# A written order of 800 steps, ordered anew: linear attention and a channel mix on one core

## The chip, the cores and the metric

The kernel runs on one core of a Trainium2 chip. The metric is the device time of one execution in microseconds. The kernel before took 197.18 us (median of three runs, 197.18 to 197.22).

## The reference, cut to what matters

```python
def _attn_ref(q, k, v, g_norm):            # q, k, v: (8, 8, 576, 64) = batch, head, token, channel
    kv = np.einsum('bhsd,bhse->bhde', k, v)
    out = np.einsum('bhsd,bhde->bhse', q, kv)
    rms = np.sqrt(np.mean(out * out, axis=-1, keepdims=True) + 1e-06)
    return out / rms * g_norm

def _moe_ref(x, mu_k, mu_r, w_k, w_v, w_r):  # x: (8, 576, 512), w_k: (512, 1024), w_v: (1024, 512), w_r: (512, 512)
    x_prev = np.concatenate([np.zeros((B, 1, D)), x[:, :-1, :]], axis=1)
    xk = mu_k * x + (1.0 - mu_k) * x_prev
    xr = mu_r * x + (1.0 - mu_r) * x_prev
    k = np.maximum(xk @ w_k, 0.0)
    v = k * k @ w_v
    r = 1.0 / (1.0 + np.exp(-(xr @ w_r)))
    return r * v

def reference(**kwargs):                   # x is the attention's output, heads side by side in the channels
    ...
```

## The kernel before

Every batch goes through two halves. The attention half makes `kv` from k and v, turns q, multiplies them (`u`), squares and reduces the result, takes a reciprocal root (`rs`), multiplies by it, and turns the result into `xT`, with channels on the partitions. The channel-mix half forms the difference of neighbouring tokens (`dx`), scales it by `mu_k` or `mu_r` (`m`), adds `x` (`xk`, `xr`), and runs three large products: `K` (`xk` by `w_k`, relu, square), `R` (`xr` by `w_r`, sigmoid) and `V` (the squares by `w_v`). Two batches together make nine tiles of 128 tokens for `R` and `V`.

The order of all this is written out by hand or by a search: `ORDER` is one list of some 800 words, and a loop at the end of the kernel calls one function for each (`name.arguments`). A planner takes no part (`manual_schedule`); each engine runs its instructions in the list's order, and waits where data or a buffer isn't ready. An apostrophe puts the step on VectorE (DVE), otherwise it goes to ScalarE (ACT), where there is a choice. Digits behind `=` choose the PSUM banks that the step takes, of eight; a bank is taken again only after the step that empties it.

The words that matter below:

- `cast`, `kvc`, `kvco`, `qtc`, `qtco`, `uc`, `sqc`, `msc`, `rsc`, `mcc`: the attention half of batch 0, which has code of its own (cast the first loads; kv on TensorE (PE) and its evacuation; q's transposes and their evacuation; the product; its square; the means by a matmul; the root; the product with the root into `xT`).
- `cols`: a transpose of the rows with `mu_k`, `mu_r` and `g_norm` into columns, and its copy on DVE.
- `wm.n.i`: n matmuls on zeros into a bank that nobody reads; they keep PE busy. Another 12 stand ahead of the list.
- `dif`, `difh`, `dih`: the difference; `sc`: the scale by `mu` (`sc.b.0.h` for `xk`, `sc.b.1.h` for `xr`); `fu`: scale and addition in one; `add`, `adda`: the addition.
- `Ka`, `Kz`: `K` of batch 0's later tokens, in two halves of the contraction; `Kz` ends with the relu. `Kp.b.j.n`: `K` for other parts of batches 0 and 1 (`Kp.0.1` are the "low units", the first 256 tokens of batch 0). `K.b.f.h`: from batch 2 on. `ksp`, `ks`: the square of the relu's result.
- `qt`, `qto`, `kvh`, `kvho`, `uh`, `sqh`, `redh`, `rsh`, `mulh`, `xh`, `xho`, `x0h`, `x0ho`: batch 1's attention, in two halves of the heads (the last digit, 0 or 1).
- `kv`, `kvo`, `kvs`, `u`, `sq`, `red`, `nw`, `mul`, `x`, `xo`, `x0`, `x0o`, `wrap`: the attention of later batches; `qd` and `yd`: transposes by DMA on SP's queue, from batch 3 and 4 on; `gx`: the scale by `g_norm`.
- `R`, `V`, `Vq` (half a `V` step), `fin`, `fip`, `sta`, `L`: the products, their last multiplication and the stores.
- `ld.n.b`: the load of k, v or q (n = 0, 1, 2) of batch b on GpSimd's queue. The loads of batches 0 and 1 and of the weights are issued ahead of the list, in a fixed order.

```python
    for period in ORDER:
        for word in period.split():
            word, _, digits = word.partition("=")
            chosen[:] = map(int, digits)
            name, *args = word.rstrip("'").split(".")
            ops[name](DVE if word.endswith("'") else ACT, *map(int, args))
```

Of the kernel before, what the change touches and what calls it, by code (L numbers as in the profile page):

```python
# [31 lines left out]
    ld.1.2 Kp.0.1.2=1 mulh.1.1.0 xh.2.2.0=56 x0h.0=32 Kz.0.5 mulh.1.0.0 x0ho.0.1 xh.0.2.0=74 ksp.0.1.0.4'
    Vq.0.1.0=1 xho.0.2.0.0 sc.0.1.2 sc.0.1.0' xho.2.2.0.1' ksp.0.1.4.8' Vq.0.0.0=0 xho.0.2.0.1 xho.2.2.0.0'
    qt.1.1=62 kvh.1=75 qto.1.1.1 Vq.0.1.1 kvho.1.0 x0ho.0.0' qto.1.1.0' kvho.1.1 Vq.0.0.1 uh.0.1=34 ld.2.3
    ksp.0.0.4.8' uh.1.1=62 uh.2.1=7 Vq.0.3.0=5 sqh.0.1.1 add.0.1.0 sqh.0.0.1 Vq.0.3.1 ld.1.3 add.0.1.1 sqh.1.1.1
    sqh.2.0.1 sqh.1.0.1 redh.5.9.1 rsh.5.9.1 redh.0.5.1 rsh.0.5.1 Vq.0.3.2 tab ld.0.3 mulh.0.0.1 Vq.0.0.2
    mulh.0.1.1 Vq.0.3.3 Vq.0.1.2 mulh.2.0.1 Vq.0.0.3 xh.2.2.1=34 mulh.1.1.1 mulh.1.0.1 xho.2.2.1.0' xho.2.2.1.1
    Vq.0.1.3 xh.0.2.1=72 x0h.1=63 xho.0.2.1.0 xho.0.2.1.1 wrap.1 x0ho.1.0' x0ho.1.1' R.0.3=4 dif.1.384.576
    dif.1.0.384 sc.1.0.3.384.576 R.0.2=6 sc.1.0.1.0.384' sc.1.0.2.384.576' sc.1.0.1.384.576 R.0.0=3 qt.2.0=72
    sc.1.1.0' qt.2.1=46 sc.1.0.3.0.384' sc.1.0.2.0.384' sc.1.0.0.0.384' qto.2.1.0 qto.2.1.1 sc.1.0.0.384.576'  # L40
    R.0.1=3 adda.1.0.384.576 add.1.0.0.0.384 add.1.0.1.0.384 Kp.1.0.2'=4 qto.2.0.1' Kp.1.0.3'=6 Kp.1.1.1=3
    Vq.0.2.0=4 ld.2.4 fin.0.1 Vq.0.2.1 fin.0.3 sc.1.1.1 add.1.1.0 Vq.0.2.2 Kp.1.1.2=2 qto.2.0.0' fin.0.0
    sc.1.1.3' Vq.0.2.3 qd.3 sc.1.1.2' Kp.1.1.3'=6 Kp.1.1.0=3 Kp.1.1.5'=1 kv.2=57 ksp.1.1.0.2 kvo.2.0' kvo.2.1'
    Kp.1.1.4=2 u.2.2=0 u.2.1=63 sq.2.2.0 add.1.1.1 sq.2.1.0 u.2.0=15 sq.2.1.1 Kp.1.0.0=7 sq.2.0.0 sq.2.0.1 qd.4
    ksp.1.1.2.4' ld.0.4 ld.1.4 Kp.1.1.7=2 fin.0.2 red.2.0.5 R.1.4=4 red.2.5.9 Kp.1.1.6=7 Kp.1.0.1=2 R.1.5=4
    ksp.1.1.4.6' ld.2.5 nw.2.0.1 V.1.5.0=7 nw.2.1.2 nw.2.2.3 ksp.1.1.6.8 nw.2.3.4 nw.2.4.5 R.1.7=2 V.1.4.0=4
# [8 lines left out]
    K.2.1.1=0 nw.3.2.3 sc.2.1.1' K.2.4.1=3 K.2.4.0=6 nw.3.3.4 K.2.7.0=0 nw.3.4.5 ks.2.5' K.2.1.0=3 nw.3.5.6
    sc.2.1.2 nw.3.6.7 nw.3.7.8 mul.3.1.1 mul.3.2.0 K.2.6.0=6 ks.2.1 K.2.6.1=0 V.1.8.0=3 K.2.2.1=6 mul.3.1.0
    K.2.3.0=5 mul.3.0.1 mul.3.0.0 add.2.1.1 add.2.1.0 K.2.2.0'=1 K.2.7.1=0 K.2.0.0=7 x0.3=65 ks.2.6 x.3.0.4=42
    V.1.8.1 xo.3.0.4.1 x0o.3.1 R.2.0=0 ks.2.3 xo.3.0.4.0' ks.2.2' x0o.3.0' ks.2.4' wrap.3 R.2.3=7 ks.2.7 R.2.2=1
    ks.2.0' dif.3 sc.3.0.3' sc.3.0.1 V.2.0.0=4 kv.4=25 V.2.2.0=6 V.2.2.1 fin.1.8 sc.3.1.3' kvo.4.1' sc.3.0.0'
# [7 lines left out]
    K.3.2.0=7 ks.3.7' ks.3.1' kvo.5.1 add.3.1.1 V.2.3.0=1 K.3.5.0=6 K.3.6.0=2 V.2.3.1 yd.4 kvs.5.1 K.3.5.1=3
    ks.3.2' kvs.5.0 sc.3.1.1' K.3.3.1=5 K.3.3.0=7 u.5.0=06 sq.5.0.1 sq.5.0.0 fin.2.1 u.5.1=24 u.5.2=3 sq.5.1.0
    sq.5.2.0 add.3.1.0 fin.2.3 sq.5.1.1 R.3.6=1 R.3.4=5 ks.3.3' R.3.8=7 V.3.7.0=1 ks.3.6' red.5.5.9 red.5.0.5
    nw.5.0.1 V.3.6.0=5 ks.3.5 ld.0.6 nw.5.1.2 nw.5.2.3 nw.5.3.4 nw.5.4.5 nw.5.5.6 nw.5.6.7 V.3.6.1 nw.5.7.8  # L70
    mul.5.2.0 gx.4.1 mul.5.1.0 V.3.7.1 V.3.4.0=7 ld.1.6 mul.5.1.1 gx.4.0 mul.5.0.0 R.3.5=3 mul.5.0.1 wrap.4
# [770 lines left out]
```

## Time and profile before

| | |
|---|---|
| median of three runs | 197.18 us |
| the profiled execution's own time | 197.49 us |
| its span, first to last instruction | 195.7 us |
| TensorE busy | 186.0 us, 2316 records of matmuls |
| VectorE busy | 160.1 us, 349 instructions |
| ScalarE busy | 133.8 us, 279 instructions |
| GpSimd busy | 30.7 us |
| moved by DMA | 32.75 MB, mean 167 GB/s |

A busy share is time in which at least one instruction of the engine was under way. Matmuls overlap: one of 512 columns shows 379 ns, and twenty in a row take 4.3 us. A few matmul records are missing from the trace, so counts in the groups are a little low. A row of the timeline gives start, length, engine, line, operation, output and inputs, count, and in brackets the idle time of the engine ahead of it and what ended it. Columns of the table of stretches: length, then busy time and count of PE, PE's weight loads, DVE, ACT and GpSimd, then granted clock, DMA share and GB/s.

### The profile page before, as it was taken

The numbers are of one execution on the slowest core, as the hardware profiler recorded it, in microseconds if no ns is written. First come the engines' busy times: TensorE is split into PE (matmuls) and PEld (weight loads), VectorE is DVE, ScalarE is ACT, GpSimd is POOL, SyncE is SP. The second block draws the span as 40 slices with busy tenths as digits, with TensorE's granted clock in tenths as the row PEclk, the third lists the DMA queues.
The fourth block names the chain that finished last, engine by engine and source line by source line (L and its number), as shares of the span: only waits on it lengthen the run. The fifth ranks groups of instructions, "written<-read, shape, count | busy, mean of one in ns | idle before, by whom it ended". The sixth has DMA issues, their size and how long they took to land.

```text
span 195.7 us, 5668 instructions
## 1 busy us (share of the span) xinstructions
PE 186.0 (95%) x2316; PEld 110.5 (56%) x2343; DVE 160.1 (82%) x349; ACT 133.8 (68%) x279; POOL 30.7 (16%) x50
## 2 busy tenths in 40 slices
...
GB/s 220 212 211 205 195 208 205 208 209 230 233 177 166 147 224 228 206 246 211 183 169 141 188 173 160 225 179 85 186 169 73 87 138 0 54 55 109 54 153 170
DMA packets 42958, 32.75 MB, mean 167 GB/s; under 512 B 23852, under 2 KB 37428, under 8 KB 42932
## 3 DMA queue, kind: packets, MB, share of 16 engines
...
## 4 chain that ended last, share of the span: by engine, by line
PE 56%; DVE 30%; ACT 5%; issue 3%; DMA 3%; SPq 1%; DVEq 0%
PE ps_km L634 21%; PE ps_v L676 17%; PE ps_r L666 11%; DMA rows<-in_g_norm_dram 3%; DVE yd L401 3%; DVE sqk L642 2%; DVE xr L621 2%; PE ps_kv L288 1%; DVE y__1281 L423 1%; PE ps_km L725 1%; DVE xT L515 1%; DVE ss__1215 L363 1%; PE ps_u L318 1%; DVE ss__2860 L363 1%; DVE ss__1583 L363 1%
## 5 line engine op out<-in xcount | busy, mean ns | idle before, releaser
L676 PE MATMUL ps_v<-wv_sb,sqk 128*128 128x512 bf16 x265 | 64.4, 379 | 1.4 <-issue 0.8
L634 PEld LDWEIGHTS <-wk_sb 128*128 128x128 bf16 x480 | 45.8, 98 | 16.8 <-issue 0.5
L676 PEld LDWEIGHTS <-sqk 128*128 128x128 bf16 x280 | 26.6, 98 | 28.8
L666 PE MATMUL ps_r<-wr_sb,xr 128*128 128x512 bf16 x135 | 35.2, 379 | 0.6
L666 PEld LDWEIGHTS <-xr 128*128 128x128 bf16 x144 | 13.8, 98 | 14.3 <-DVE xr L621 0.2
L626 ACT ACTIVATE rt<-ps_km 128x384 bf16<-128x384 f32 (+2 forms) x18 | 8.8, 506 | 7.0 <-PE ps_km L634 4.2
L261 PE MATMUL ps_warm<-zeros 128*128 128x512 bf16 x25 | 9.4, 501 | 1.2 <-DVE eps L224 1.2
L634 PE MATMUL ps_km<-xk__3239,wk_sb 128*128 128x288 bf16 x64 | 9.0, 286 | 0.0
L634 PE MATMUL ps_km<-xk__968,wk_sb 128*128 128x192 bf16 (+1 forms) x64 | 8.8, 286 | 0.0
L634 PE MATMUL ps_km<-xk__2666,wk_sb 128*128 128x288 bf16 x64 | 8.8, 286 | 0.0
L634 PE MATMUL ps_km<-xk__3386,wk_sb 128*128 128x288 bf16 x64 | 8.7, 286 | 0.1
L634 PE MATMUL ps_km<-xk__2429,wk_sb 128*128 128x288 bf16 x64 | 8.7, 286 | 0.0
L634 PE MATMUL ps_km<-xk__1923,wk_sb 128*128 128x288 bf16 x64 | 8.7, 286 | 0.0
L634 PE MATMUL ps_km<-xk__1557,wk_sb 128*128 128x288 bf16 x64 | 8.4, 286 | 0.1
L428 ACT ACTIVATE xT<-xT,cols 128x1152 bf16<-128x1152 bf16 x6 | 7.3, 1266 | 0.1
L515 DVE SCALAR_TENSOR_TENSOR xT<-ps_u,cols,rs 128x384 bf16<-128x384 f32 x6 | 3.7, 613 | 3.1 <-ACT rs L511 3.1
L725 PE MATMUL ps_km<-xk__371,wk_sb 128*128 128x320 bf16 x32 | 5.4, 299 | 0.7 <-DVE xk__371 L610 0.4
L261 PEld LDWEIGHTS <-zeros 128*128 128x128 bf16 x28 | 3.0, 117 | 5.0 <-issue 3.1
...
L428 ACT ACTIVATE xT<-ps_x,cols 128x256 bf16<-128x256 bf16 (+3 forms) x10 | 5.2, 563 | 0.4 <-PE ps_x L438 0.4
...
L642 DVE TENSOR_TENSOR sqk<-rt 128x1280 bf16<-128x1280 bf16 (+3 forms) x7 | 5.1, 722 | 0.0
...
## 6 DMA issues: line engine op xcount, KB each, us to landing
...
```

The lines of the kernel that those rows point to most:

```text
L261: nc.tensor.matmul(ps, zeros[:, :128], zeros, start=True, stop=True)
L363: DVE.tensor_reduce(out=ss[:, g0:g1], in_=sq[:, g0:g1], op=ALU.add, axis=AX.X)
L401: DVE.tensor_mul(out=pairs[:, :, i, 1 + t0:1 + t0 + n].rearrange("p c t x -> p t c x"), in0=u_, in1=by)
L428: eng.activation(out=dst, in_=src, func=AF.Copy, scale=g_sb)
L515: DVE.scalar_tensor_tensor(out=xT[0][:, hps, P + c0:P + c1], in0=give(("uc", key)), scalar=g_sb, in1=rs0[:, hps, c0:c1], op0=ALU.mult, op1 ...
L621: DVE.tensor_add(out=dst, in0=m[:, hs, c0:c1], in1=x[:, hs, c0:c1])
L626: eng.activation(out=dst, in_=ps, func=AF.Relu)
L634: nc.tensor.matmul(ps[:, n, :], wk_sb[:, cc, 128 * fc:128 * fc + 128], at[b]["xk"][:, cc, c0:c1], start=(cc == 0), stop=(cc == NHP - 1))
L642: eng.tensor_mul(out=sqk[:, fcs, o:o + n], in0=src, in1=src)
L666: nc.tensor.matmul(ps, xr[:, cc, 128 * t:128 * t + 128], wr_sb[:, cc, :], start=(cc == 0), stop=(cc == NHP - 1))
L676: nc.tensor.matmul(ps, sqk[:, fc, 128 * t:128 * t + 128], wv_sb[:, fc, :], start=(fc == 0), stop=(fc == NFC - 1))
L725: nc.tensor.matmul(ps[:, n, :], wk_sb[:, cc, 128 * fc:128 * fc + 128], at[0]["xk"][:, cc, c0:c1], start=(cc == 0), stop=(cc == NHP - 1))
```

## The change

Only `ORDER` differs. The same steps stand in another order, with other banks, and some steps change between DVE and ACT (60 go to DVE, 58 to ACT over the whole list). No matmul, no other operation and no load is added or taken away but for the warming matmuls: 28 before, 26 after. The loads that stand in the list change places within it: v of batch 2 now goes ahead of k of batch 2, k of batch 3 ahead of v of batch 3, and so on. Line numbers below the list grow by one.

The start of the list, before and after (the rest is ordered anew in the same manner, up to the last two steps, `L.0` and `L.1`):

```diff
-    cast.1' cast.0 kvc.0.2=01 cols=2 kvco.0 qtc.0.2=34 kvco.1 qtco.0' qtco.1 wm.2.0=2 uc.0=5 qtc.2.2=67
+    cast.0' cast.1' kvc.0.2=01 kvco.0 wm.1.0=7 qtc.0.2=23 kvco.1' qtco.0' qtco.1 cols=4 wm.1.1=1 uc.0=5 sqc.0
+    uc.1=6 qtc.2.2=70 msc.0=1 sqc.1 msc.1=2 wm.1.2=3 kvc.2.1=4 kvco.2' qtco.2 rsc.0 wm.1.3=1 uc.2=3 rsc.1 uc.4=7
+    qtco.3' wm.1.4=0 kvc.3.1=1 kvco.3 sqc.2 wm.1.5=0 uc.3=4 mcc.1 mcc.0 difh.0.0.256.576 sc.0.0.0.256.576' sqc.3
+    uc.5=2 sqc.5 msc.2=0 sc.0.0.1.256.576' rsc.2 wm.1.6=1 msc.3=6 rsc.3 sqc.4 msc.5=5 ld.2.2 add.0.0.0.256.576
+    mcc.2 dih.0.2.256.576 wm.4.7=1 Ka.0.7=1 msc.4=0 rsc.4 Ka.0.4=6 mcc.3 fu.0.0.2.256.576 dih.0.3.256.576
+    Ka.0.6=3 Ka.0.5=4 fu.0.0.3.256.576 Ka.0.0=0 rsc.5
...
-    sqc.0 uc.1=0 ld.2.2 sqc.1 qtco.2 msc.0=1 wm.2.1=4 msc.1=2 rsc.0 kvc.2.1=3 kvco.2 wm.2.2=6 uc.2=4 uc.4=6
-    rsc.1 mcc.1 qtco.3' mcc.0 difh.0.0.256.576 kvc.3.1=1 sqc.2 sqc.4 sc.0.0.1.256.576' sc.0.0.0.256.576' msc.2=3
-    kvco.3 wm.1.3=0 uc.3=2 msc.4=0 uc.5=1 sqc.3 rsc.4 msc.3=7 add.0.0.0.256.576 wm.4.4=5 Ka.0.0=5 rsc.3 sqc.5
-    mcc.3 Ka.0.5=0 rsc.2 dih.0.3.256.576 mcc.2 fu.0.0.3.256.576 mcc.4 msc.5=7 rsc.5 Ka.0.4=2 Ka.0.6=3 Ka.0.2=4
-    dih.0.2.256.576 fu.0.0.2.256.576 mcc.5 Ka.0.1=7 wrap.0 difh.0.0.0.256 Ka.0.7=6 difh.0.1.0.256 fu.0.0.3.0.256
-    Kz.0.4 Kz.0.0 Kz.0.1' Ka.0.3=1 Kz.0.3' fu.0.0.1.0.256 Kz.0.6 wm.2.5=5 qt.1.0=25 qto.1.0.1 Kz.0.2 Kz.0.7
-    fu.0.0.2.0.256 wm.2.6=1 kvh.0=37 kvho.0.1 qto.1.0.0' sc.0.1.1' kvho.0.0' fu.0.0.0.0.256 wm.1.7=6 uh.0.0=15
-    uh.1.0=42 sqh.0.1.0 sqh.1.1.0 sc.0.1.3' uh.2.0=6 ksp.0.0.0.4' sqh.0.0.0 sqh.1.0.0 sqh.2.0.0 redh.5.9.0
...
+    ld.1.2 Ka.0.3=5 Kz.0.0 mcc.5 Kz.0.4 Kz.0.6 Kz.0.5 Ka.0.1=2 wrap.0 mcc.4 Kz.0.3 difh.0.0.0.256 difh.0.1.0.256
+    fu.0.0.3.0.256 fu.0.0.1.0.256 Kz.0.7 fu.0.0.2.0.256 fu.0.0.0.0.256 sc.0.1.1 Ka.0.2=0 Kz.0.2 Kz.0.1'
+    qt.1.0=76 sc.0.1.3 qto.1.0.0 wm.1.8=1 Kp.0.1.1=3 qto.1.0.1' sc.0.1.2 kvh.0=45 ksp.0.0.0.4' kvho.0.1'
+    kvho.0.0' wm.2.9=7 uh.2.0=1 sqh.2.0.0 uh.1.0=02 uh.0.0=67 sqh.1.1.0 ksp.0.0.4.8' sqh.1.0.0 sc.0.1.0'
+    redh.0.5.0 sqh.0.0.0 Kp.0.1.0=5 sqh.0.1.0 ksp.0.1.0.4' rsh.0.5.0 mulh.2.0.0 redh.5.9.0 Kp.0.1.3=3 mulh.1.0.0
+    Kp.0.1.2=4 mulh.1.1.0 Vq.0.1.0=5 Vq.0.1.1 Vq.0.0.0=1 xh.0.2.0=34 rsh.5.9.0 ksp.0.1.4.8' qt.1.1=02
+    xho.0.2.0.0' mulh.0.1.0 xho.0.2.0.1 mulh.0.0.0 add.0.1.1 qto.1.1.1 x0h.0=34 qto.1.1.0 Vq.0.0.1 kvh.1=76
+    ld.0.2 x0ho.0.0' kvho.1.1' xh.2.2.0=20 ld.2.3 x0ho.0.1' xho.2.2.0.0' xho.2.2.0.1' kvho.1.0 uh.0.1=37
+    add.0.1.0 uh.1.1=64 uh.2.1=2 Vq.0.0.2 sqh.0.0.1 Vq.0.3.0=0 sqh.0.1.1 sqh.1.1.1 sqh.1.0.1 sqh.2.0.1
...
```

More of the change, by code (lines that the diff above doesn't have):

```diff
@@ L32 @@
[L32 to L46, printed above, removed]
@@ L55 @@
[L55 to L59, printed above, removed]
@@ L67 @@
[L67 to L71, printed above, removed]
@@ new lines @@
+    add.0.1.0 uh.1.1=64 uh.2.1=2 Vq.0.0.2 sqh.0.0.1 Vq.0.3.0=0 sqh.0.1.1 sqh.1.1.1 sqh.1.0.1 sqh.2.0.1
+    redh.5.9.1 Vq.0.1.2 redh.0.5.1 Vq.0.3.1 rsh.5.9.1 Vq.0.1.3 Vq.0.3.2 rsh.0.5.1 Vq.0.0.3 mulh.0.0.1 tab
+    mulh.0.1.1 mulh.1.0.1 xh.2.2.1=37 Vq.0.3.3 ld.0.3 mulh.1.1.1 ld.1.3 xho.2.2.1.0 mulh.2.0.1 xh.0.2.1=64
+    xho.2.2.1.1' xho.0.2.1.0' xho.0.2.1.1 x0h.1=27 x0ho.1.0' dif.1.384.576 R.0.2=3 wrap.1 sc.1.0.0.384.576
+    R.0.1=6 R.0.3=4 sc.1.0.2.384.576 x0ho.1.1' dif.1.0.384 R.0.0=2 qt.2.0=73 qt.2.1=64 sc.1.0.1.0.384 sc.1.1.1
@@ new lines @@
+    sc.1.0.0.0.384' ld.2.4 sc.1.0.1.384.576' sc.1.0.3.0.384' sc.1.0.3.384.576' Vq.0.2.0=2 sc.1.0.2.0.384'
+    adda.1.0.384.576 fin.0.1 add.1.0.1.0.384 Vq.0.2.1 qto.2.1.1' Kp.1.0.3=5 add.1.0.0.0.384 Kp.1.0.2'=4 sc.1.1.0
+    Vq.0.2.2 sc.1.1.2 qto.2.1.0 sc.1.1.3' Vq.0.2.3 Kp.1.1.1=5 qto.2.0.0' fin.0.2 fin.0.0 Kp.1.1.7=4 kv.2=76
+    add.1.1.1 qto.2.0.1' kvo.2.0 kvo.2.1 add.1.1.0 Kp.1.1.2=2 u.2.0=51 u.2.2=4 sq.2.0.1 Kp.1.1.5=7 fin.0.3
+    sq.2.0.0 qd.3 Kp.1.1.4=6 Kp.1.1.0=3 u.2.1=20 red.2.5.9 sq.2.1.0 ksp.1.1.0.2' sq.2.2.0 Kp.1.1.3'=7 sq.2.1.1
@@ new lines @@
+    fin.1.7 sc.2.0.2' V.1.6.0=3 sc.2.0.1' u.3.0=70 sq.3.0.0 add.2.0.1 u.3.2=1 sq.3.2.0 fin.1.4 u.3.1=45
+    add.2.0.0 sq.3.1.0 sq.3.1.1 V.1.6.1 add.2.1.0
+    """,
+    """
+    K.2.4.1=6 K.2.0.0=2 fin.1.6 red.3.0.5 K.2.3.1=3 sq.3.0.1 K.2.1.0=6 K.2.0.1=2 K.2.1.1=3 sc.2.1.3' red.3.5.9
+    K.2.3.0'=6 nw.3.0.1 nw.3.1.2 sc.2.1.2 K.2.2.1=2 nw.3.2.3 nw.3.3.4 K.2.7.1=3 nw.3.4.5 nw.3.5.6 K.2.5.1=6
+    K.2.4.0=2 V.1.8.0=3 nw.3.6.7 ks.2.0 K.2.7.0=6 K.2.2.0=2 ks.2.4 nw.3.7.8 V.1.8.1 ks.2.3 ks.2.1 mul.3.1.1
```

88 lines of the change are left out of this document (47 added, 41 removed).

## The prediction

> **What bounds the kernel now.** I read the page's busy shares first, then the list of waits for TensorE (PE) alone from 31.35 us to 192 us, then the table of stretches. The span is 195.7 us.
>
> ```profile
> span 195.7 us, 5668 instructions
> ...
> PE 186.0 (95%) x2316; PEld 110.5 (56%) x2343; DVE 160.1 (82%) x349; ACT 133.8 (68%) x279; POOL 30.7 (16%) x50
> ```
>
> ```profile
> PE ps_v L676 <- issue: 0.6, 4, 0.2
> PE ps_v L676 <- DVE out__3051 L689: 0.2, 1, 0.2
> ```
>
> ```profile
> 31.35:50.00 18.65, 18.45 (x297) 10.77 (x296) 17.33 (x43) 13.47 (x30) 1.55 (x3) 1.00 1.21 218
> 50.00:75.00 25.00, 24.46 (x347) 15.29 (x351) 24.35 (x51) 19.45 (x43) 6.16 (x8) 1.00 1.09 190
> ```
>
> PE is busy 95% of the span, and from 31.35 us to the end of its work it waited 0.8 us in all (0.6 + 0.2). Behind 31.35 us the old order is work of PE from end to end, at a granted clock of 1.00. VectorE (DVE) is close behind (24.35 of 25.00 us), ScalarE (ACT) is not (19.45).
>
> This gives the frame of the whole prediction. In the old list the step `Vq.0.3.0` starts at 31.35 us. In the new list, the PE steps that stand ahead of `Vq.0.0.2` are, apart from the warming matmuls, exactly the same set: all of `Ka`, `Kz`, the four `Kp.0.1`, batch 1's `qt`, `kvh` and `uh`, its first `xh` and `x0h`, and four `Vq`. Behind these two points each list holds the same 253 PE steps and no warming matmul. So the new kernel can gain in three places only: when it comes to `Vq.0.0.2`, how often PE changes between large and small matmuls after it, and the 0.8 us of waits, of which it can take away at most all. It can lose wherever a new wait arises.
>
> **Term 1: the time of the common point.** Three parts of the change act here.
>
> First, `cols` (the transpose of the scale columns) now stands behind `qtc.0.2`. These are the rows of PE at the start:
>
> ```profile
> 6.88 0.48 PE L475 MATMUL ps_kv<-rt 64*64 64x64 bf16 x36 [0.38 <-DVE rt L219]
> 8.03 0.20 PE L588 MATMUL ps_cols<-rows_id,rows 9*128 9x9 f32 x1 [0.67 <-DMA rows<-in_g_norm_dram]
> 8.15 0.48 PE L484 MATMUL ps_qt<-ident,q 64*64 64x64 bf16 x36
> ```
>
> In the old order the query transposes waited behind `cols` for the rows' DMA, 0.67 us. In the new order one warming matmul stands there, and `cols` waits later, beside other work. I take 0.5 us sooner for the transposes (bounds 0 and 0.67).
>
> Second, DVE's and ACT's order in batch 0. DVE's rows:
>
> ```profile
> 8.68 0.46 DVE L219 COPY qT<-ps_qt 128x576 bf16<-128x576 bf16 x1 [0.25 <-PE ps_qt L484]
> 12.20 0.62 DVE L515 SCALAR_TENSOR_TENSOR xT<-ps_u,cols,rs 128x384 bf16<-128x384 f32 x1 [3.07 <-ACT rs L511]
> 12.74 0.45 DVE L219 COPY qT<-ps_qt 128x576 bf16<-128x576 bf16 x1
> 13.10 0.61 DVE L515 SCALAR_TENSOR_TENSOR xT<-ps_u,cols,rs 128x384 bf16<-128x384 f32 x1
> ...
> 24.47 1.41 DVE L553 TENSOR_REDUCE ss__569<-sq__556 128x8 f32<-128x512 bf16 x2
> 25.80 1.61 DVE L563 TENSOR_TENSOR y__584<-ps_u,rs__582 128x256 bf16<-128x256 f32 x5
> 27.32 0.68 DVE L642 TENSOR_TENSOR sqk<-rt 128x1024 bf16<-128x1024 bf16 x1
> 27.92 0.37 DVE L606 TENSOR_SCALAR m__530<-dx__326,cols 128x576 bf16<-128x576 bf16 x1
> 28.20 0.35 DVE L430 TENSOR_SCALAR xT<-ps_x,cols 128x256 bf16<-128x256 bf16 x1
> ```
>
> From the copy's end (9.14) to the first product (12.20) DVE sat idle 3.07 us, on ACT. With the copy 0.5 us sooner the product comes at 11.7. The copy `qtco.3`, which took 0.36 us between two products (12.74 to 13.10), now goes into that idle time; `cast.0` and two `kvco`, so far on ACT, go into DVE's idle time of the start as well. So the first half of batch 0 is ready about 0.9 us sooner (0.5 + 0.36).
>
> Third, ACT gets work between batch 0's relus and batch 1's squares. Its rows, and PE's at the end of this part:
>
> ```profile
> 19.06 0.77 ACT L626 ACTIVATE rt<-ps_km 128x320 bf16<-128x320 f32 x2 [2.08 <-DVE xT L515]
> ...
> 23.50 1.38 ACT L548 ACTIVATE sq__556<-ps_u 128x256 bf16<-128x256 f32 x5 [0.37 <-PE ps_u L543]
> 24.76 0.61 ACT L626 ACTIVATE rt<-ps_km 128x512 bf16<-128x512 f32 x1
> 25.26 0.30 ACT L557 ACTIVATE rs__582<-ss__569,eps 128x8 f32<-128x8 f32 x1
> ...
> 28.90 0.78 ACT L604 ACTIVATE m__530<-dx__326,cols 128x576 bf16<-128x576 bf16 x1
> 29.57 0.48 ACT L428 ACTIVATE xT<-ps_x,cols 128x256 bf16<-128x256 bf16 x1
> 29.92 0.65 ACT L217 COPY qT__439<-ps_qt 128x576 bf16<-128x576 bf16 x1
> ```
>
> ```profile
> 29.45 0.48 PE L525 MATMUL ps_kv<-in_v,in_k 64*64 64x64 bf16 x36
> 30.09 0.81 PE L676 MATMUL ps_v<-wv_sb,sqk 128*128 128x512 bf16 x3 [0.16 <-issue]
> 30.83 0.59 PE L543 MATMUL ps_u<-kv__489,qT__439 64*128 64x64 bf16 x20
> 31.35 3.19 PE L676 MATMUL ps_v<-wv_sb,sqk 128*128 128x512 bf16 x14
> ```
>
> The old ACT list has three relus, a copy, two relus and a small cast here. The new one, in order: six relus (0.39 each, half of the 0.77), the scale `sc.0.1.1` (0.78), a relu, the scale `sc.0.1.3` (0.78), the copy `qto.1.0.0` (0.65), the relu of `Kp.0.1.1` (0.61), the scale `sc.0.1.2` (0.78), and only then the first square of batch 1. On DVE a scale costs 0.37. From 18.2 (19.06 less the 0.9) that makes 18.2 + 2.3 + 0.78 + 0.39 + 0.78 + 0.65 + 0.61 + 0.78 = 24.5; neighbours overlap a little (the pair of relus shows 0.77 for two), so 24.3. Now the squares start at 23.50. The lead of 0.9 us is gone and turned into 0.8 us of delay on this chain.
>
> From there: three squares (0.28 each) to 25.1, a reduction (0.71) to 25.85, on DVE a part square (0.68) to 26.5, a product (0.32), the second reduction (0.71) to 27.55, two products (0.64), a part square (0.68), an `xho` scale (0.35) and the two products that free banks 7 and 6 (0.64) to 29.85. `kvh.1` takes these two banks, so it starts near 29.7 by this chain (29.45 now). It cannot start before its values land:
>
> ```profile
> L213 POOL DMA_DIRECT2D in_v<-in_v_dram x1: 716/716/716, 15.4 to 15.4; - x1
> ...
> DMA to landing us min/median/max: 13.7/13.7/13.7
> ```
>
> The load issued at 15.4 landed at 29.1, and all loads up to this one stand in the same place in both kernels. From `kvh.1` to `uh.0.1` took 1.38 us (29.45 to 30.83) with 0.81 us of `Vq` between them; the new list has nothing but `xh.2.2.0` there, but two copies of 0.65 stand before the evacuation on ACT, so I take 1.05 (bounds 0.6 and 1.4). `uh` takes 0.5 (30.83 to 31.35). So `Vq.0.0.2` starts at 29.7 + 1.05 + 0.5 = 31.25: **-0.1 us**. Bounds: 30.7, with `kvh.1` at the landing and the rest alike, to 32.0, with the whole 0.8 us of ACT's delay added: -0.65 to +0.7 us.
>
> The two warming matmuls that go (28 before, 26 after) lie ahead of this point, in time that the chains leave open: nothing. Without that cover they would be worth two matmuls of the 14 that took 3.19 us: 0.45.
>
> **Term 2: changes of matmul size behind it.** I counted in both lists how often a step of large matmuls is followed by small ones: 17 times before, 18 after (`u.2.1` is split off from the other two `u.2` by three `Kp`).
>
> ```profile
> 77.99 1.03 PE L676 MATMUL ps_v<-wv_sb,sqk 128*128 128x512 bf16 x4
> 78.94 0.78 PE L288 MATMUL ps_kv<-qT,sq 64*64 64x64 bf16 x72
> 79.88 1.67 PE L676 MATMUL ps_v<-wv_sb,sqk 128*128 128x512 bf16 x7 [0.16 <-issue]
> ```
>
> From the start of one large group to the next is 1.89 us (77.99 to 79.88). Four large matmuls issue in 0.86, the 72 small ones in about 0.7: one change there and back costs some 0.3 us. **+0.3 us.** Bounds 0.2 and 0.4.
>
> **Edits costed at nothing.** Loads: `ld.1.2` now goes ahead of `ld.0.2`, and likewise further on. `kv` waits for both tensors, so the pair's last landing counts, and the queue carries the same bytes. The cover is the distance to `kv.2`, which moves up about 3 us in the list; if that cover is gone, PE waits there for the later half, which I hold against the forecast under the rivals. The store of `fin.0.2` now goes ahead of the transposes on SP's queue: two issues more before `qd.3`; `qd.4` waits for its load anyway. Behind the common point 21 steps up to `kv.4` move from DVE to ACT and 17 the other way. The last steps of PE are the same two `L`.
>
> [...] In the stretch from 5 to 10 us PE is only partly busy, warming included, and the granted clock stayed at 1.00.
>
> ```profile
> 5.00:10.00 5.00, 3.71 (x118) 2.04 (x118) 1.39 (x3) 2.08 (x5) 4.07 (x9) 1.00 1.20 210
> ```
>
> [...]
>
> **Sum.** -0.1 + 0.3 = +0.2 us on the profiled execution's own 197.49 us: 197.7. The median of the three runs is 197.18 us, 0.3 lower, so the forecast is 197.4 us. A measurement of this kernel tells 0.2% (0.4 us) from no change.
>
> **Rivals.**
>
> *The start's gain comes through (faster).* `kvh.1` starts at the landing, 29.1, the point moves by -0.65, and half or all of the 0.8 us of old waits goes: -0.65 + 0.3 - 0.4 = -0.75 us, 196.4 us; with all of them 196.0. For it: DVE's idle 3.07 us is real and is filled. Against: the three scales that ACT gets. Chance 0.25.
>
> *ACT delays batch 1 (slower).* The place is the row of scales ahead of `sqh.2.0.0`. If the squares start later than 24.3, everything up to `uh.0.1` moves with them, since each step in that chain waits for the one before. Price: one scale's 0.78 us, +0.7 + 0.3 = +1.0 us, 198.2 us. For it: ACT works strictly in its order, and a relu that waits for PE holds the scale behind it. Chance 0.24.
>
> *PE waits for late evacuations in the later stages (slower).* ACT's free time is 5.2 us in 31.35:50 and 5.55 us in 50:75 (18.65 - 13.47, 25.00 - 19.45). It takes four steps more than it gives; at 0.4 to 0.8 us each (the relu's and the scale's durations above) that is 1.6 to 3.2 us. There is room on the mean, but a bank that is freed 0.5 us late stops PE for 0.5 us. With one such place per two batches, and `kv.2` coming to its load early, +0.5 to +1.7 us: 197.9 to 199.1. It decides if PE's list of waits behind the common point shows more than 1.3 us. Chance 0.2.
>
> *The change doesn't do what it says.* [...] Chance 0.01.
>
> **How the numbers follow.** The forecast, no change that can be told, has 0.3; its own range is 197.0 to 197.6 us. Faster by over 0.2%: 0.25. Slower by over 0.2%: 0.24 + 0.2 + 0.01 = 0.45. The range that leaves out two in ten goes from the middle of the first rival, 196.4, to near the end of the third, 198.8.
>
> **What would show it.** Right: `Vq.0.0.2` on PE between 31.0 and 31.6; DVE's first product of batch 0 near 11.7; ACT's first `sqh` near 24.3; PE's waits behind 31 us still below 1.3 us. Wrong: squares before 23.7 and `Vq.0.0.2` before 30.9 (first rival); `Vq.0.0.2` behind 31.8 (second); PE waits of more than 1.3 us behind it (third).

## The result and the profile after

The changed kernel takes 198.98 us (median of six runs, 198.70 to 199.13), the kernel before 197.20 us in the same group. The ratio over all executions is 1.0076, 95% interval 1.0050 to 1.0102: slower by 0.8% (by the medians 0.9%; two of the six executions of the kernel before took 198.30 and 198.91 us). The profiled execution took 199.1 us, with a span of 197.3 us against 195.7.

From the page of the changed kernel, PE's busy time:

```profile
span 197.3 us, 5687 instructions
...
PE 188.2 (95%) x2341; PEld 110.4 (56%) x2341; DVE 159.5 (81%) x351; ACT 132.8 (67%) x277; POOL 29.4 (15%) x50
```

PE's waits over the whole span, and a stretch behind the common point (the prediction's `Vq.0.0.2`, from which both lists hold the same work for PE):

```profile
PE ps_kv L476 <- DVE rt L220: 1.5, 1, 1.5
PE ps_warm L262 <- DVE eps L225: 1.2, 1, 1.2
PE ps_km L726 <- DMA wk_sb<-in_moe_w_k_dram: 0.2, 1, 0.2
```

```profile
31.35:50.00 18.65, 18.65 (x294) 10.62 (x292) 15.98 (x38) 15.25 (x34) 1.04 (x2) 1.00 1.20 224
```

All three waits lie in the first 18 us. Behind the common point PE waits for nothing; in the stretch shown it is busy for 18.65 of 18.65 us. The old 0.8 us of waits are gone. Nothing here says slower. PE's rows at the common point:

```profile
28.62 0.60 PE L677 MATMUL ps_v<-wv_sb,sqk 128*128 128x512 bf16 x2
29.35 0.48 PE L526 MATMUL ps_kv<-in_v,in_k 64*64 64x64 bf16 x36
29.76 0.29 PE L439 MATMUL ps_x<-ident,y__601 64*128 64x64 bf16 x8
30.14 0.72 PE L544 MATMUL ps_u<-kv__508,qT__453 64*128 64x64 bf16 x20
30.79 1.68 PE L677 MATMUL ps_v<-wv_sb,sqk 128*128 128x512 bf16 x7
```

`Vq.0.0.2` starts at 30.79 us; the old list was at its common point at 31.35. That is 0.56 us sooner. DVE's last product starts at 191.82 us, 192.07 before (rows below), and PE's first matmul of `L.0` shows the same 0.25 us (189.87 against 190.12). So the changed kernel is 0.25 us ahead when its arithmetic ends, and 1.6 us behind when its span ends. The loss lies in the last 5 us, on ACT. Here are the last product on DVE and ACT with its DMA queue (ACTq: issue of a store, start and length), of the kernel before and then of the changed one:

```profile
192.07 0.36 DVE L689 TENSOR_TENSOR out__3724<-ps_v,sig__3695 128x192 f32<-128x192 f32 x1
187.60 0.56 ACTq L699 DMA_DIRECT2D out_dram<-out__3670  x1
190.32 0.60 ACT L669 ACTIVATE sig__3695<-ps_r 128x512 bf16<-128x512 f32 x1 [5.45 <-PE ps_r L666]
190.39 0.48 ACTq L699 DMA_DIRECT2D out_dram<-out__3697  x1
190.91 0.62 ACTq L699 DMA_DIRECT2D out_dram<-out__3674  x1
191.99 0.50 ACTq L699 DMA_DIRECT2D out_dram<-out__3711  x1
192.59 0.80 ACTq L699 DMA_DIRECT2D out_dram<-out__3724  x1
```

```profile
191.82 0.36 DVE L690 TENSOR_TENSOR out__3724<-ps_v,sig__3594 128x192 f32<-128x192 f32 x1 [0.17 <-PE ps_v L685]
189.21 0.60 ACT L670 ACTIVATE sig__3686<-ps_r 128x512 bf16<-128x512 f32 x1 [5.54 <-PE ps_r L667]
189.55 2.70 ACTq L700 DMA_DIRECT2D out_dram<-out__3670  x1
192.28 0.78 ACTq L700 DMA_DIRECT2D out_dram<-out__3658  x1
193.16 0.56 ACTq L700 DMA_DIRECT2D out_dram<-out__3697  x1
193.82 0.55 ACTq L700 DMA_DIRECT2D out_dram<-out__3711  x1
194.47 0.56 ACTq L700 DMA_DIRECT2D out_dram<-out__3724  x1
```

From the end of the last product to the end of the span (the tail, from here on) it was 3.27 us (192.43 to 195.7); it is 5.12 us (192.18 to 197.3). Every other store of ACT issues in 0.5 to 0.8 us; one takes 2.70 us, and four stand behind it. The lists differ there in this, which the diff shown above does not reach (`sta` is ACT's half of a store, `R` the last sigmoid, for which ACT waits 5.5 us):

```diff
-    R.7.7=3 fin.6.1 ks.7.6 V.7.5.0=7 R.7.5=0 V.7.4.1 V.7.6.0=1 fin.7.4 V.7.6.1 V.7.5.1 fip.7.6 sta.7.6 fip.7.5
-    V.7.7.0=6 fin.6.0 V.7.7.1 R.7.8=4 fip.7.7 sta.7.7 sta.7.5 L.0=3 L.1=0
...
+    fip.7.6 V.7.5.1 V.7.4.0=7 fip.7.5 V.7.4.1 fin.6.1 R.7.7=0 sta.7.5 V.7.7.1 fin.7.4 fip.7.7 sta.7.6 sta.7.7
+    L.0=1 L.1=5
```

Before, one `sta` stood ahead of the last sigmoid; now none does. Something else lies in that spot. In the DMA traffic of 190.40 to 191.00 us of the changed kernel one packet is of another kind than data:

```profile
q14 instruction: 1, 0.01, 5.3%
```

It is a load of instructions, one packet of 8 KB, from 190.45 to 190.96 us by the packet's own record. The page lists eight of them on this queue (q14) in the whole span. In the kernel before the last one lies at 189.85 us, while ACT still waits for PE. So there were two suspects: the place of the stores behind the sigmoid, and the instruction load.

### The profile page after: what moved, and what is told of

It is laid out like the page before. It is cut to its first block, busy times and chain, and to the rows that moved or that the text cites. A ratio compares the mean times of both kernels' runs of the same rounds, so it can differ in the third digit from the quotient of the medians.

```text
span 197.3 us, 5687 instructions
## 1 busy us (share of the span) xinstructions
PE 188.2 (95%) x2341; PEld 110.4 (56%) x2341; DVE 159.5 (81%) x351; ACT 132.8 (67%) x277; POOL 29.4 (15%) x50
## 4 chain that ended last, share of the span: by engine, by line
PE 84%; DMA 5%; DVE 4%; POOL 3%; issue 1%; POOLq 0%; DVEq 0%
PE ps_km L635 30%; PE ps_v L677 28%; PE ps_r L667 16%; DMA wk_sb<-in_moe_w_k_dram 5%; PE ps_kv L289 2%; PE ps_u L319 2%; PE ps_km L726 1%; POOL rt L184 1%; PE ps_x L439 1%; PE ps_v L685 1%; PE ps_qt L333 1%; POOL q L184 1%; DVE dx__1431 L599 1%; PE ps_u L544 1%; DVE xT L431 1%
## 5 line engine op out<-in xcount | busy, mean ns | idle before, releaser
L677 PE MATMUL ps_v<-wv_sb,sqk 128*128 128x512 bf16 x280 | 65.8, 379 | 0.0
L635 PEld LDWEIGHTS <-wk_sb 128*128 128x128 bf16 x480 | 45.7, 98 | 15.8 <-DVE xk__1507 L622 0.4
L667 PE MATMUL ps_r<-wr_sb,xr 128*128 128x512 bf16 x144 | 34.2, 379 | 0.0
L627 ACT ACTIVATE rt<-ps_km 128x384 bf16<-128x384 f32 (+2 forms) x20 | 9.3, 497 | 3.1 <-PE ps_km L635 1.5
L262 PE MATMUL ps_warm<-zeros 128*128 128x512 bf16 x26 | 8.8, 442 | 1.2 <-DVE eps L225 1.2
L635 PE MATMUL ps_km<-xk__1879,wk_sb 128*128 128x288 bf16 x64 | 8.8, 286 | 0.0
L635 PE MATMUL ps_km<-xk__1507,wk_sb 128*128 128x288 bf16 x64 | 8.7, 286 | 0.1
L635 PE MATMUL ps_km<-xk__2430,wk_sb 128*128 128x288 bf16 x64 | 8.5, 286 | 0.0
L635 PE MATMUL ps_km<-xk__3439,wk_sb 128*128 128x288 bf16 x64 | 8.5, 286 | 0.0
L635 PE MATMUL ps_km<-xk__2669,wk_sb 128*128 128x288 bf16 x64 | 8.3, 286 | 0.0
L635 PE MATMUL ps_km<-xk__3241,wk_sb 128*128 128x288 bf16 x64 | 8.2, 286 | 0.0
L431 DVE TENSOR_SCALAR xT<-ps_x,cols 128x256 bf16<-128x256 bf16 (+3 forms) x15 | 5.4, 387 | 0.9 <-PE ps_x L439 0.9
L429 ACT ACTIVATE xT<-xT,cols 128x1152 bf16<-128x1152 bf16 x4 | 4.9, 1255 | 0.0
L196 POOL COPY passed<-xT 1x2 bf16<-1x2 bf16 x2 | 0.7, 358 | 26.8 <-DMA xT<-yd 26.5
L726 PEld LDWEIGHTS <-wk_sb 128*128 128x128 bf16 x32 | 3.0, 97 | 2.3 <-DMA wk_sb<-in_moe_w_k_dram 1.0
L670 ACT ACTIVATE sig__3686<-ps_r 128x512 bf16<-128x512 f32 x1 | 0.6, 597 | 5.5 <-PE ps_r L667 5.5
```

Of the source, the lines that this page charges most:

```text
L262: nc.tensor.matmul(ps, zeros[:, :128], zeros, start=True, stop=True)
L429: eng.activation(out=dst, in_=src, func=AF.Copy, scale=g_sb)
L431: eng.tensor_scalar(out=dst, in0=src, scalar1=g_sb, scalar2=None, op0=ALU.mult)
L627: eng.activation(out=dst, in_=ps, func=AF.Relu)
L635: nc.tensor.matmul(ps[:, n, :], wk_sb[:, cc, 128 * fc:128 * fc + 128], at[b]["xk"][:, cc, c0:c1], start=(cc == 0), stop=(cc == NHP - 1))
L667: nc.tensor.matmul(ps, xr[:, cc, 128 * t:128 * t + 128], wr_sb[:, cc, :], start=(cc == 0), stop=(cc == NHP - 1))
```

## The experiments

Medians and ratios to the kernel before (95% interval), and the last instruction load and the tail (end of DVE's last product to end of span) of each profiled execution:

| kernel | us | ratio | last load at | tail, us |
|---|---|---|---|---|
| changed kernel | 198.98 | 1.0076 (1.0050 to 1.0102) | 190.45 | 5.1 |
| e1: both stores ahead of the sigmoid | 197.08 | 0.9986 (0.9971 to 1.0001) | 187.72 | 3.3 |
| e2: kernel before, store behind | 197.82 | 1.0026 (1.0010 to 1.0041) | 184.98 | 3.9 |
| e3: eight tiny instructions more | 197.31 | 0.9999 (0.9983 to 1.0015) | 183.05 | 3.7 |
| e12: one tiny instruction more | 197.37 | 0.9988 (0.9960 to 1.0016) | 183.41 | 3.6 |
| e11: one store ahead | 197.05 | 0.9957 (0.9931 to 0.9982) | 187.64 | 3.3 |
| e9: four instructions fewer | 197.48 | 1.0002 (0.9985 to 1.0019) | 193.06 | 3.7 |
| e10: six fewer | 197.47 | 1.0006 (0.9997 to 1.0016) | 193.23 | 3.7 |

**e1: the two stores ahead of the sigmoid.**

```diff
-    fip.7.6 V.7.5.1 V.7.4.0=7 fip.7.5 V.7.4.1 fin.6.1 R.7.7=0 sta.7.5 V.7.7.1 fin.7.4 fip.7.7 sta.7.6 sta.7.7
+    fip.7.6 sta.7.6 V.7.5.1 V.7.4.0=7 fip.7.5 sta.7.5 V.7.4.1 fin.6.1 R.7.7=0 V.7.7.1 fin.7.4 fip.7.7 sta.7.7
```

> The changed kernel with two stores of ACT's queue moved: sta.7.6 goes right behind fip.7.6 and sta.7.5 right behind fip.7.5, both ahead of the last sigmoid R.7.7. PE ended 0.25 us sooner after the change, and the span ended 1.6 us later. Theory A (the end is lost on ACT's queue: the stores stand behind the last sigmoid, and the first of them takes 2.70 us there): ACT sits idle for 5.5 us ahead of that sigmoid, so the moved stores are free; from the end of the last DVE product to the end of the span 3.2 to 3.4 us as before the change (3.27), the whole 0.25 us under the kernel before: 196.9 us. Theory B (the end is late for another reason, such as the load of the DMA engines or SP's queue): the time stays near 198.9 us.

197.08 us, 1.9 us under the changed kernel and 0.1 us under the kernel before. ACT and its queue:

```profile
185.46 0.55 ACTq L700 DMA_DIRECT2D out_dram<-out__3658  x1
187.13 0.50 ACTq L700 DMA_DIRECT2D out_dram<-out__3671  x1
188.99 0.60 ACT L670 ACTIVATE sig__3688<-ps_r 128x512 bf16<-128x512 f32 x1 [5.54 <-PE ps_r L667]
```

The two stores lie in ACT's idle time, and the tail is 3.3 us again. The loss is the tail's, and it hangs on ACT's queue: theory B is out.

**e2: the kernel before with its early store behind the sigmoid.**

```diff
-    ... V.7.5.1 fip.7.6 sta.7.6 fip.7.5
-    V.7.7.0=6 fin.6.0 V.7.7.1 R.7.8=4 fip.7.7 sta.7.7 sta.7.5 L.0=3 L.1=0
+    ... V.7.5.1 fip.7.6 fip.7.5
+    V.7.7.0=6 fin.6.0 V.7.7.1 R.7.8=4 sta.7.6 fip.7.7 sta.7.7 sta.7.5 L.0=3 L.1=0
```

> The kernel before with one step moved: sta.7.6, the only store that ACT issued ahead of the last sigmoid, goes right behind that sigmoid, as all of them stand in the changed kernel. Theory A in its simple form (what counts is that the first store stands behind the sigmoid): that first store takes some 2.7 us and the end comes later by 1.0 to 1.9 us, 198.2 to 199.1 us. Theory A by number only (each store behind the sigmoid costs its 0.55 us of issue): +0.5 us, 197.7 us. Theory C (the 2.70 us are a load of the next piece of ACT's instructions, whose packet of 8 KB the trace shows at 190.45 us in the changed kernel and at 189.85 us in the kernel before, and which comes at a fixed count of instructions): here the store is one instruction later on ACT than the same load, so it depends on that one place; the load falls either on the first or the second store, between +0.3 and +1.9 us. Theory B: 197.2 us.

197.82 us, 0.57 us more than the kernel before in its group (197.25). The sigmoid and the first store behind it:

```profile
189.96 0.60 ACT L669 ACTIVATE sig__3694<-ps_r 128x512 bf16<-128x512 f32 x1 [5.45 <-PE ps_r L666]
190.02 0.56 ACTq L699 DMA_DIRECT2D out_dram<-out__3670  x1
```

Five stores behind the sigmoid, as in the changed kernel, and the first takes 0.56 us; the last load lies at 184.98 us, in ACT's idle time. The place alone doesn't make 2.70. It makes about one issue: ACT's last issue ends 1.60 us behind the last product, 0.96 us in the kernel before.

**e3 and e12: tiny instructions ahead of the sigmoid.** The stores stay where the changed kernel has them; ACT gets eight, or one, activations of 128x1 in its idle 5.5 us.

```diff
-    ... fin.6.1 R.7.7=0 sta.7.5 ...
+    ... fin.6.1 pad.8 R.7.7=0 sta.7.5 ...      (e12: pad.1)
...
+        "pad": lambda eng, n: [ACT.activation(out=pads, in_=cols[:, 0:1], func=AF.Copy) for _ in range(n)],
```

> The changed kernel with eight tiny activations (128x1 each, output unused) on ACT ahead of the last sigmoid, in its idle 5.5 us; the stores stay behind the sigmoid. Theory A in its simple form (the first store on ACT's queue takes 2.7 us when it stands behind the sigmoid): nothing changes, first store 2.7 us, 198.9 us. Theory C (the load of ACT's next piece of instructions comes at a fixed count): eight instructions more put that load into the idle time ahead of the sigmoid, its 8 KB packet comes near 185 to 186 us, the first store takes 0.5 to 0.8 us, and the time falls by 1.3 to 2.0 us, to 197.0 to 197.6 us. Theory B: 198.9 us.

> The changed kernel with one tiny activation (128x1, output unused) on ACT ahead of the last sigmoid, instead of the eight of e3; all stores stay behind the sigmoid. Theory C3: one place is enough, the load falls on the wait ahead of the sigmoid, packet between 184 and 190 us, first store 0.5 to 0.8 us, 197.2 to 197.6 us, as e3 (197.31). Theory C2 or A: packet near 190.4 us and the first store 1.5 to 2.8 us still, 198.3 to 199.0 us.

197.31 and 197.37 us: more work on ACT, and 1.6 us less time. The rows of e12, and the one instruction packet that the trace shows between 183.40 and 184.05 us:

```profile
183.21 0.20 ACT L782 ACTIVATE pads__119<-cols 128x1 f32<-128x1 f32 x1
188.87 0.60 ACT L671 ACTIVATE sig__3688<-ps_r 128x512 bf16<-128x512 f32 x1 [5.45 <-PE ps_r L668]
188.93 0.56 ACTq L701 DMA_DIRECT2D out_dram<-out__3671  x1
```

```profile
q14 instruction: 1, 0.01, 5.8%
```

One instruction of 0.20 us more moves the load from 190.45 to 183.41 us, into the idle time, and the first store falls from 2.70 to 0.56 us. The stores stand as in the changed kernel, so their order is not what makes the 1.6 us; one place on ACT's list is. The load moves with that place, and so I take the load for what held the store. That it did the holding is not shown by itself: the 2.70 us stand in one kernel, and no other run put a load on a store of ACT. What is left over e1 (tails of 3.6 and 3.7 against 3.3 us, 197.37 and 197.31 against 197.08) is the price of the order alone, 0.2 to 0.3 us. It is not a longer queue of issues: ACT's last issue ends 0.91 us behind the last product in e12, 0.90 in e1. The last store's landing took longer, 2.5 us from its issue against 2.2; why, no run shows.

**e11: one store ahead, one behind.**

```diff
-    fip.7.6 V.7.5.1 ... R.7.7=0 sta.7.5 V.7.7.1 fin.7.4 fip.7.7 sta.7.6 sta.7.7
+    fip.7.6 sta.7.6 V.7.5.1 ... R.7.7=0 sta.7.5 V.7.7.1 fin.7.4 fip.7.7 sta.7.7
```

> The changed kernel with only sta.7.6 moved ahead of the last sigmoid, right behind fip.7.6; sta.7.5, sta.7.7 and the last two stay behind the sigmoid. sta.7.5 is again the first store behind the sigmoid, but no longer ACT's first store, and it stands one or two places later than the 2.70 us store of the changed kernel. Theory C3 (only the instruction at which the instruction load falls due is held, until some 1.3 us behind the load's packet): the load falls on the sigmoid or beside it, no store takes over 0.8 us, 197.1 to 197.4 us. Theory C2 (any store issued between the call for the load and its packet is held): sta.7.5 takes 1.5 to 2.8 us, 198.0 to 198.7 us. Theory A (the first store behind the last sigmoid takes 2.7 us when nothing else moved the load): as C2.

197.05 us. `sta.7.5` is again the first store behind the sigmoid:

```profile
185.38 0.55 ACTq L700 DMA_DIRECT2D out_dram<-out__3658  x1
188.91 0.60 ACT L670 ACTIVATE sig__3687<-ps_r 128x512 bf16<-128x512 f32 x1 [5.54 <-PE ps_r L667]
188.98 0.49 ACTq L700 DMA_DIRECT2D out_dram<-out__3671  x1
```

It takes 0.49 us; the load came at 187.64, in the wait. So a store can be the first behind the sigmoid and cost nothing more. Between the two forms of theory C the run does not decide, since no store was under way near the load. e1 says more: its store from 187.13 to 187.63 us ended 0.1 us ahead of the packet (187.72) and was not held, which speaks against every store near a load being held.

**e9 and e10: the load pushed later.** On e1, four scales of the last batch (in e10 two squares as well) move from ACT to DVE:

```diff
-    sc.7.1.1 ... sc.7.1.0 ... sc.7.1.2 ... sc.7.1.3 ... ks.7.3 ... ks.7.0
+    sc.7.1.1' ... sc.7.1.0' ... sc.7.1.2' ... sc.7.1.3' ... ks.7.3' ... ks.7.0'      (ks in e10 only)
```

> The changed kernel with the stores moved as e1, and the four scales sc.7.1.0 to sc.7.1.3 of the last batch moved from ACT to DVE, into its idle time there: ACT has four instructions fewer ahead of its stores. In e5, with three fewer, the 8 KB packet of an instruction load came at 190.04 us, between the last sigmoid (189.46) and the store sta.7.7 (191.10), and touched no store. Theory C2 (a load of ACT's instructions comes at a fixed count, and a store that is being issued while it is under way takes some 2 us more): with one place more it falls on sta.7.7: packet between 190.6 and 191.8 us, one of the stores sta.7.7 and L.0 on ACT takes 1.5 to 2.8 us, from the last product on DVE to the end of the span 4.2 to 5.0 us instead of 3.3, 198.0 to 198.7 us, with every store where e1 has it. Rival (the 2.70 us belonged to the first store behind the last sigmoid): no store over 0.8 us, 197.1 us.

> As e9, and two squares of the last batch (ks.7.3, ks.7.0) moved from ACT to DVE as well: six instructions fewer ahead of the stores. Theory C2: the packet comes two places later than in e9, near 191.3 to 192.6 us, on one of the last two stores (L.0, L.1), which takes 1.5 to 2.8 us; from the last product to the end of the span 4.0 to 5.2 us; 198.0 to 198.9 us if the squares on DVE delay nothing. If instead the load falls behind the last store, nothing is seen and the end is as in e1, 3.3 us. Rival (first store behind the sigmoid): no store over 0.8 us, 197.1 us.

Both missed. I wanted the load on another store; it came at 193.06 and 193.23 us, behind the last one. ACT's queue in e9:

```profile
190.66 0.50 ACTq L700 DMA_DIRECT2D out_dram<-out__3698  x1
191.53 0.50 ACTq L700 DMA_DIRECT2D out_dram<-out__3711  x1
192.13 0.75 ACTq L700 DMA_DIRECT2D out_dram<-out__3724  x1
```

No store was held. The tail grew to 3.7 us all the same, and the medians are 0.4 us over e1. The load among the last landings is not shown to be the reason: in e9 the last store landed 2.6 us after its issue, and in e3, whose load came 10 us earlier, 2.5 us, with the same tail. And two places more (e10 against e9) did not move the load against the stores, so a bare count of instructions is not its whole rule.

**e5: the three scales back on DVE** (on e1).

```diff
-    ... fu.0.0.0.0.256 sc.0.1.1 Ka.0.2=0 ... qt.1.0=76 sc.0.1.3 ... sc.0.1.2 kvh.0=45
+    ... fu.0.0.0.0.256 sc.0.1.1' Ka.0.2=0 ... qt.1.0=76 sc.0.1.3' ... sc.0.1.2' kvh.0=45
```

> The changed kernel with the stores moved ahead of the last sigmoid (as e1), and the three scales sc.0.1.1, sc.0.1.3 and sc.0.1.2 given back to DVE: ACT has three instructions fewer from 19 us on, and everything on ACT comes three places sooner. At the start, theory of the prediction (the scales on ACT delay batch 1's squares and with them the common point): the first square starts 0.8 to 2 us before 23.4 us and the common point moves ahead of 30.67 us by 0.3 us or more. Rival (the landing of the values at 29.1 us sets the start of kvh.1): squares sooner, the common point within 0.2 us of 30.67. At the end, theory C (a load of ACT's next instructions at a fixed count, near record 319 of the trace in all four runs with stores in different places): it now falls on the store sta.7.7, which stands three places further on; packet of 8 KB near 191 us, that store takes 2 to 2.7 us instead of 0.50, and the span ends 1.0 to 1.6 us later than in e1, 198.0 to 198.7 us, although no store has changed its place. Rival (the store took 2.70 us because it was the first behind the sigmoid): the end as in e1, 197.0 us.

197.59 us, 0.5 us over e1. ACT's squares and PE's common point:

```profile
23.93 1.18 ACT L549 ACTIVATE sq__558<-ps_u 128x128 bf16<-128x128 f32 x4 [1.07 <-PE ps_u L544]
```

```profile
31.16 1.25 PE L677 MATMUL ps_v<-wv_sb,sqk 128*128 128x512 bf16 x5
```

Both theories of the start missed. With the scales off ACT its squares came 0.5 us later, not sooner (23.93 against 23.43 in e1), after an idle 1.07 us, in which ACT waited for PE's `uh` (`ps_u`). DVE, with three scales of 0.36 us more, started its two casts of `kv` for that step at 23.24 us, 22.67 in the changed kernel; that `uh` waited for these casts is my reading, no row shows it. The common point moved by the same 0.5 us (30.67 to 31.16). At the end theory C missed too: the load fell at 190.04 us, between the sigmoid and `sta.7.7`. That store was issued at 191.10 us in 0.50 us, and the tail was 3.4 us.

**e6: `cols` back ahead of `qtc.0.2`** (on e1).

```diff
-    wm.1.0=7 qtc.0.2=23 kvco.1' qtco.0' qtco.1 cols=4 wm.1.1=1
+    wm.1.0=7 cols=4 qtc.0.2=23 kvco.1' qtco.0' qtco.1 wm.1.1=1
```

> The changed kernel with the stores moved as e1, and the step cols back ahead of qtc.0.2, where it stood before. Theory of the prediction's first part (qtc comes 0.5 us sooner through this move, and with it DVE's first product): qtc.0.2 near 8.0 us instead of 7.5, DVE's first product mcc.1 near 11.8 instead of 11.3. What it is worth at the common point: if the chain of batch 0 carries it, +0.4 to +0.6 us there and 197.6 us; if the landing of the values at 29.1 us sets kvh.1, less than 0.2 us and 197.1 us. No change at the end by any theory: ACT's count of instructions is the same.

`qtc.0.2` went from 7.50 to 7.89 us, DVE's first product from 11.33 to 11.72, the squares from 23.43 to 23.62, the common point from 30.67 to 30.83, the time from 197.08 to 197.22 us. Of 0.39 us at the start 0.16 us reach the common point.

**e7: the two `Vq` back behind `kvh.1`** (on e1).

```diff
-    Vq.0.1.0=5 Vq.0.1.1 Vq.0.0.0=1 ... qto.1.1.0 Vq.0.0.1 kvh.1=76 ... kvho.1.0 uh.0.1=37
+    Vq.0.1.0=5 Vq.0.0.0=1 ... qto.1.1.0 kvh.1=76 ... kvho.1.0 Vq.0.1.1 Vq.0.0.1 uh.0.1=37
```

> The changed kernel with the stores moved as e1, and the two steps Vq.0.1.1 and Vq.0.0.1 moved from ahead of kvh.1 to behind it, ahead of uh.0.1, where they stood before the change. Theory D (the common point came 0.56 us sooner because these 0.8 us of work now fill PE's wait for the values' landing instead of coming behind it): kvh.1 stays at 29.2, uh.0.1 goes from 29.86 to 30.5 to 30.8, the common point to 31.2 to 31.5, 197.6 to 197.9 us. Theory of the prediction's sum (the point is set by the chain of batch 1 on ACT and DVE, and these steps lie beside it): within 0.2 us of e1, 197.1 us.

197.91 us, 0.8 us over e1. PE:

```profile
29.17 0.48 PE L526 MATMUL ps_kv<-in_v,in_k 64*64 64x64 bf16 x36 [0.55 <-DMA in_v<-in_v_dram]
...
31.29 1.25 PE L677 MATMUL ps_v<-wv_sb,sqk 128*128 128x512 bf16 x5
```

`kvh.1` starts at 29.17 us, 29.23 in e1, but now PE waits 0.55 us for the values, and the common point is at 31.29 instead of 30.67. Work that stood behind the landing of the values now fills the wait for it, and that alone is worth 0.62 us, as much as the whole gain of 0.56. It is not the only part: e5 and e6 lose 0.49 and 0.16 us at the point when they give theirs back. The three make 1.27 us, so they overlap or other edits at the start cost the rest; which of the two was not tested.

**e4: one change of matmul size fewer** (on e1).

```diff
-    ... Kp.1.1.2=2 u.2.0=51 u.2.2=4 sq.2.0.1 Kp.1.1.5=7 fin.0.3 sq.2.0.0 qd.3 Kp.1.1.4=6 Kp.1.1.0=3 u.2.1=20 ...
+    ... Kp.1.1.2=2 Kp.1.1.5=7 Kp.1.1.4=6 Kp.1.1.0=3 u.2.0=51 u.2.2=4 fin.0.3 u.2.1=20 sq.2.0.1 sq.2.0.0 qd.3 ...
```

> The changed kernel with the stores moved as in the first run of this group, and in batch 2 the three Kp that stood between u.2.2 and u.2.1 moved ahead of u.2.0, and fin.0.3 ahead of u.2.1 (it frees that step's bank): one change of matmul size fewer on PE. Theory of the prediction (such a change costs about 0.3 us): 0.3 us (0.2 to 0.4) under the first run of this group. Rival (the change of size was hidden in the weight loads or the evacuations): the same time as that run, within 0.1 us; or later by up to 0.5 us, if PE then waits for the evacuation of the three Kp one after another or for batch 2's chain, whose u come some 1.8 us later.

197.82 us, 0.7 us over e1 instead of 0.3 under it. A new wait on PE, and the row that follows it:

```profile
50.92 0.82 PE L635 MATMUL ps_km<-xk__970,wk_sb 128*128 128x192 bf16 x8 [0.76 <-DVE rt L629]
51.58 0.59 PE L667 MATMUL ps_r<-wr_sb,xr 128*128 128x512 bf16 x2
```

In e1 the same first `R` starts at 50.80 us. Without the 0.76 us the stretch would end at 50.82, so the saved change of size gave nothing that can be seen. The `u` between the `Kp` had covered DVE's evacuation (the `rt` of the row above).

**e8: the last tile cut at 384 columns** (on e1).

```diff
-        c = (slice(0, 5 * C // 8), slice(5 * C // 8, C))[part]
+        c = (slice(0, 3 * C // 4), slice(3 * C // 4, C))[part]
```

> The changed kernel with the stores moved as e1, and the last tile's two parts cut at 384 columns instead of 320: the last product on DVE is 128x128 instead of 128x192 (0.36 us) and its two stores carry 32 KB instead of 48. If the end is a chain of last product, store issue and landing: 0.05 to 0.15 us under e1, 196.95 us. If the first part's stores end it instead: the same time, or up to 0.1 us more.

197.20 us, not under e1's 197.08: the last product ended sooner (191.71 against 191.96 us), the span did not (195.3 both). On ACT's queue the last store stands behind the first part's, which was issued at 191.54 instead of 191.47 us, and so it started at 192.13 us, 192.11 in e1.

## Why the forecast was right on the side by luck and wrong on the reason

The forecast was 197.4 us, with slower as the likelier side; measured are 198.98 us, just above the range's end of 198.8 (the ratio of 1.0076 on the 197.18 us on record gives 198.68, just inside). The kernel is slower by a mechanism that was not in the forecast, and none of the rivals that were to make it slower occurred. That the likelier side came true is luck.

*The step that failed.* "The last steps of PE are the same two `L`" stood among the edits costed at nothing. True of PE; but the list also orders ACT's stores around the last sigmoid, and the end of the span hangs on ACT's queue, not on PE. Of that +1.85 us in the tail, about 1.6 us are the held first store (198.98 us against 197.37 and 197.31 with the load moved away), and 0.2 to 0.3 us the stores' place behind the sigmoid (e12 and e3 against e1). The first part could not be read from the diff. The second could have had a bound: one store more behind the sigmoid, at the 0.56 us that an issue takes in the rows of the kernel before. e2 prices that step there at 0.57 us.

*The frame.* Waits behind the common point went from 0.8 us to none, and PE came to `L.0` 0.25 us sooner: gain only through the common point, changes of size and old waits, as the frame said. The frame's wrong part was to take PE's time for the kernel's.

*Term 1, -0.1 us.* Measured -0.56, near the lower bound of -0.65. The first part held: `qtc` 0.67 us sooner (0.5 taken; 8.15 to 7.48), DVE's first product at 11.35 (11.7 taken). The second failed: ACT's squares at 24.3 were in truth at 23.44, 0.06 us sooner than before. ACT's rows:

```profile
18.11 2.12 ACT L627 ACTIVATE rt<-ps_km 128x320 bf16<-128x320 f32 x6 [1.18 <-PE ps_km L726]
20.11 0.78 ACT L605 ACTIVATE m__442<-dx__352,cols 128x576 bf16<-128x576 bf16 x1
20.78 0.44 ACT L627 ACTIVATE rt<-ps_km 128x320 bf16<-128x320 f32 x1
...
22.77 0.80 ACT L605 ACTIVATE m__442<-dx__352,cols 128x576 bf16<-128x576 bf16 x1
23.44 1.12 ACT L549 ACTIVATE sq__558<-ps_u 128x128 bf16<-128x128 f32 x4
```

A scale shows 0.78 us, but the next instruction starts 0.67 us behind it (20.11 to 20.78). The sum of lengths made 6.3 us; the starts make 5.33 (18.11 to 23.44). Adding lengths where starts should be added cost 0.9 us, the whole delay that I had forecast for the squares. e5 shows the sign was wrong too: with the scales on DVE the squares came at 23.93 us and the time was 197.59 us, against 23.43 and 197.08 in e1. The third part was mis-sized too: `kvh.1` at 29.35 us, close behind the landing (15.4 + 13.8), where 29.7 was taken (the chain as added up there gives 29.85). From there to `uh.0.1` it was 0.79 us (29.35 to 30.14; 1.05 taken), and `uh` took 0.65 (0.5 taken). Together that is the 0.46 us by which the point came before the forecast's 31.25. Both `Vq` had gone ahead into the wait; e7 gives them back and loses 0.62 us at the point.

*Term 2, +0.3 us.* From the common point to `L.0` PE takes 159.08 us (30.79 to 189.87) against 158.77 (31.35 to 190.12): +0.31, with no waits left in it. In e1, e11 and e12, where PE's order is the same, it takes 158.98, 159.01 and 158.90 us: +0.1 to +0.2. The size fits roughly, the cause is not shown: e4 takes the extra change away and saves nothing. Where that time sits stays open.

*Edits at nothing, and the warming matmuls.* Load order, the store of `fin.0.2`, steps to ACT: there is no wait behind the common point, so they cost PE nothing. With two warming matmuls fewer PE was less busy from 5 to 10 us (3.34 us, 3.71 before), and the granted clock held at 1.00:

```profile
5.00:10.00 5.00, 3.34 (x120) 2.08 (x118) 1.79 (x5) 1.94 (x5) 4.67 (x10) 1.00 1.20 210
```

*The rivals.* The first one's marks were met, squares before 23.7 and the point before 30.9, and its gain is there, 0.25 us at `L.0` and 0.1 us in e1's time; its price of -0.75 was too high. ACT's delay of batch 1 did not occur (squares at 23.44 us, not behind 24.3), nor did late evacuations: no PE wait behind the point. For the fourth, with its chance of 0.01, the profiles of the kernel before and of the changed one show no slower clock under PE's work: 1.00 in every stretch shown.

*The best version* is the change's new start with the old tail: e1 and e11, 197.08 and 197.05 us, against 197.25 to 197.45 for the kernel before in the groups with these experiments. By the medians the gain is 0.1 to 0.2%, and for e1 the interval reaches 1.
